# Output product of a two-layer expert chain: direct 128x512 matmuls against seven block products with column halves of 256

## The chip, the cores and the metric

The kernel runs on one core of a Trainium2 chip. The metric is the time of one execution on the device in microseconds (us); the median of the runs is compared. Engines are named as in the profile: PE (TensorE matmul), PEld (TensorE weight load), DVE (VectorE), ACT (ScalarE), POOL (GpSimd), SP (SyncE, which issues most of the DMAs).

## The reference

```python
x = attention(q, k, v, mem_k, mem_v)          # windows of 32 queries, 4 x 8 x 768 x 64
x = x.transpose(0, 2, 1, 3).reshape(3072, 512)
y = ((x @ w1) * (x @ w2) @ w3) @ w_out        # d_ff 1024
return ((y @ w_a) * (y @ w_b)) @ w_out2       # d_ff 1536, w_out2 is 1536 x 512
```

All in float32. The change is to the very last product, `@ w_out2`, 3072 x 1536 by 1536 x 512.

## The kernel before, in words

Tokens lie in 6 tiles of 512 (`TT`), numbered 0 to 5. A float32 product is made with three matmuls of reduced-precision operands: each factor is split into a high and a low part (high: an ACT copy that rounds, `split_hi`, L106; low: a subtraction, `split_lo`, L109), and `PASSES` runs high x high, high x low, low x high, each of them 128 rows by 512 columns.

The program has these stages. Until 389 us come the attention, the weight preparation and, for tiles 0 to 3, the first expert layer directly (psA, psB, psY). In the weight preparation the 64-bit words that the host hands over are turned into float32 (`blocks_of`, with two ACT and two DVE instructions a block, L411, L412, L416, L417). Tiles 4 and 5 go through the first layer as a pair (`seven12`): the pair's two products `x@w1` and `x@w2` are made of seven block products (two token tiles by two halves of the inner dimension by the two weight matrices), each of them 6 matmuls (L944), with the sums around them on DVE; between these, `hook()` lets a generator do preparation work. This stage runs from 389 to 509 us.

The last stage takes the token pairs (0,1), (2,3), (4,5) one after the other, 509 to 1052 us. For each pair a loop over 12 blocks of d_ff (`M2`, 128 wide) makes seven block products (`seven`, 42 matmuls), which give two gated blocks g1 (first token tile) and g2 (second). g is split by ACT and POOL (`g_rest`, L1129). `out_part` then multiplies by block f of `w_out2`, 4 row blocks x 3 passes = 12 matmuls of 128x512 (L96, `ops`): for the first token tile in the loop, one block late; for the second after the loop, 132 of its 144 matmuls in a row. The results leave PSUM by DVE and ACT copies (L1179, L1181) and four DMAs a tile. While the second tile's products run, `x_build` makes the seven sums of the next pair's x on DVE (L774) and splits them.

Each engine runs its instructions in the order in which the program text issues them; waits between engines are semaphores that the framework puts in. The weights of one block, seven quarter tiles, are loaded ahead (`w7_a`, `w7_b`) into one of two slots, by SP's queue in `seven12` and by POOL's queue in the last stage, and split by ACT and DVE (`w7_split`, `w7_lo`). `w_out2` is decoded during the first pair (`w_out_blocks`) and stays in SBUF, split, for all three pairs.

Of the kernel before, what the change touches and what calls it, by code (L numbers as in the profile page):

```python
# [47 lines left out]
def tile_attention_moe(  # L48
# [40 lines left out]
    wcd = [dram_tile(f"wc{f}", [P, W7]) for f in range(M2)]  # L89
    wdd = [dram_tile(f"wd{m}", [P, W7]) for m in range(M1)]  # L90
# [405 lines left out]
    def blocks_of(stage, src, out, bufs, raws_n=2):  # L496
# [9 lines left out]
        load()  # L506
        load()
# [29 lines left out]
    def c_weights():  # L537
        blocks = []
        src = [wab[f, :, c] for f in range(M2) for c in (1, 0)]
        conv = blocks_of(stage, src, blocks, 4, 3)  # L540
        next(conv)
        yield
        for _ in range(4):
            next(conv)
            yield
        for f in range(M2):
            b1, b0 = blocks[2 * f : 2 * f + 2]
            nc.sync.dma_start(out=wcd[f][:, 5 * CH // 2 :], in_=b1)
            b1, b0 = (b.rearrange("p (k j f) -> p k j f", k=2, j=2) for b in (b1, b0))
            nc.sync.dma_start(  # L550
                out=wcd[f][:, : CH // 2].rearrange("p (k f) -> p k f", k=2), in_=b0[:, :, 0]
            )
            sums = sums_of(b0[:, :, 0], b1[:, :, 0], b0[:, :, 1], b1[:, :, 1], wcd[f])
            for _ in range(4):
                next(sums, None)
                next(conv, None)
                yield

# [267 lines left out]
    def w7_a():  # L826
# [8 lines left out]
        (nc.gpsimd if c else nc.sync).dma_start(  # L835
# [8 lines left out]
        if c:  # L844
            x = [x[0], x[2], x[1], x[3]]
        parts.extend(t[:, :, c0:c1] for c0, c1 in x)

    def w7_b():
# [5 lines left out]
        (nc.gpsimd if n >= len(wseq) - NCD else nc.sync).dma_start(  # L854
# [129 lines left out]
    def seven12(m, w, ga, gb):  # L984
        pa, pb, pc = held[m % 2], held[2], held[3]
# [5 lines left out]
        if m > 0:  # L991
            w7_split()
        product(pc, 3, w, True)
# [8 lines left out]
        g_split()  # L1002
        product(pb, 1, w, True)
        onto(c11, pb, c11, ALU.add)
        w7_split()
        hook()
# [3 lines left out]
        hook()  # L1010
# [4 lines left out]
        hook()  # L1015

    first = [ncw[0], 0]

    def hook():
        first[1] += 1  # L1020
        while ncw[0] < first[0] + (NCW - first[0]) * min(first[1], NHOOK) // NHOOK:
            cw_step()

    NHOOK = 3 * M1 + 2 * KD - 2
    HM = M1 // 2
    psx = costack.enter_context(tc.tile_pool(name="psx", bufs=4, space=PS))
    for t in range(ND, NT1, 2):
        for h in range(2):
            gs = {}
            held[:] = [psx.tile([P, 512], F32, tag="x", name="ps7")[:, :TT] for _ in range(4)]  # L1030
# [58 lines left out]
    NS = TT // P  # L1089

    fo = []

    def w_out_blocks():
        blocks = []
        conv = blocks_of(stage2, [w2o[f] for f in range(M2)], blocks, 1)
        next(conv)
        yield
        for f in range(M2):
            for _ in range(2):
                next(conv)  # L1100
                yield
            yield
            if f < 4:
                w = cp.tile([P, 2, CH], F32R, tag="fo", bufs=4, name="fo")
            else:
                w = w_new(wpool, "wo")
            x = blocks.pop()
            split_hi(w[:, 0, :], x)
            yield
            split_lo(w[:, 1, :], x, w[:, 0, :])  # L1110
            fo.append(w)
            yield
# [6 lines left out]
    def times(x, y, g2):  # L1119
        z = tmp()  # L1120
        nc.vector.tensor_tensor(z, x, y, ALU.mult)
        gated.append((z, g2))

    gated = []
# [7 lines left out]
    def seven(w, g1, g2, other, after, lead):  # L1132
# [4 lines left out]
        g_rest()  # L1137
        product(pb, 1, w, True)
        c11 = plus(pb, s1)
        other(lead)  # L1140
# [10 lines left out]
        other(2)  # L1151
        product(pc, 5, w, False)
        c12 = plus(pc, u2)
        product(pa, 6, w, False)
        after()
        times(pa, c11, g1)
        times(c12, c22, g2)
        w7_lo()
        other(1)

    def out_part(ops, f, g2):
        for s in range(NS):
            for i, (a, b) in enumerate(PASSES):
                mm(
                    ops[s],
                    g2[:, a, P * s : P * s + P],
                    fo[f][:, b, :],
                    f == 0 and i == 0,
                    f == M2 - 1 and i == 2,
                )  # L1170

    def out_new(pool, tag):
        return [pool.tile([P, 512], F32, tag=tag, name="ops") for _ in range(NS)]

    def out_store(ops, t):
        for s in range(NS):
            ob = tmp()
            if s % 2 == 0:
                nc.vector.tensor_copy(ob, ops[s])  # L1179
            else:  # L1180
                nc.scalar.activation(ob, ops[s], AF.Copy)  # L1181
            r0 = t * TT + s * P
            nc.sync.dma_start(out=out[r0 : r0 + P, :], in_=ob)

    stagestack = ExitStack()
    stage2 = stagestack.enter_context(tc.tile_pool(name="stage2", bufs=2))
    cw = w_out_blocks()
    next(cw)

# [17 lines left out]
    for si, t in enumerate(seq):  # L1207
        nxt = seq[si + 1] if si + 1 < len(seq) else None
        g1, g2 = [], []
        spare = xs.pop().rearrange("p l k t -> p k l t")  # L1210
        ops = out_new(pso, "o")
        for f in range(M2):
            g1.append(cp.tile([P, 2, TT], F32R, tag="g1", bufs=3, name="g1"))
            if f < M2 - 2:
                g2.append(cp.tile([P, 2, TT], F32R, tag="g2", bufs=M2 - 2, name="g2"))
            else:
                g2.append(spare[:, f - M2 + 2])

            seven(w7.pop(0), g1[f], g2[f], other, w7_ab, 2 * (f > 0))
            while len(fo) < f:  # L1220
                next(cw)
            if f > 0:
                out_part(ops, f - 1, g1[f - 1])
        while len(fo) < M2:
            next(cw)
        g_rest()
        ops2 = out_new(psd, "d")
        out_part(ops2, 0, g2[0])
        out_part(ops, M2 - 1, g1[M2 - 1])
        out_store(ops, t)  # L1230
        if nxt is not None:
            xs = [x_new() for _ in range(8)]
            for _ in x_build(xs, yd, nxt):
                pass
        for f in range(1, M2):
            out_part(ops2, f, g2[f])
        out_store(ops2, t + 1)
        if si == 0:
            stagestack.close()
            cw = y_sums()  # L1240
# [83 lines left out]
```

## Time and profile before

| | |
|---|---|
| median of 3 runs | 1053.46 us (1053.05 to 1495.51) |
| profiled execution | 1053.67 us |
| its span on the core | 1051.9 us, so 1.77 us lie around it |
| granted TensorE clock, whole span | 1.00 |
| matmuls in the trace | 7402 (the program has 2288 of 128x512 on L96 and 1848 on L944) |
| last stage, three pairs | 180.0, 179.5 and 183.5 us (the last one to the end of the span) |

The page counts busy time by engine over the whole span; the stage table (windows) gives the same by stage. A matmul's mean duration in the tables runs from its issue to its modelled end and overlaps the next one; what a matmul costs in a row of them is the distance between starts, which the timeline gives.

### The profile page before, as it was taken

The numbers are of one execution on the slowest core, as the hardware profiler recorded it, in microseconds if no ns is written. First come the engines' busy times: TensorE is split into PE (matmuls) and PEld (weight loads), VectorE is DVE, ScalarE is ACT, GpSimd is POOL, SyncE is SP. The second block draws the span as 40 slices with busy tenths as digits, with TensorE's granted clock in tenths as the row PEclk, the third lists the DMA queues.
The fourth block names the chain that finished last, engine by engine and source line by source line (L and its number), as shares of the span: only waits on it lengthen the run. The fifth ranks groups of instructions, "written<-read, shape, count | busy, mean of one in ns | idle before, by whom it ended". The sixth has DMA issues, their size and how long they took to land.

```text
span 1051.9 us, 18265 instructions
## 1 busy us (share of the span) xinstructions
PE 1043.1 (99%) x7402; PEld 837.3 (80%) x7402; DVE 582.1 (55%) x896; ACT 449.2 (43%) x801; POOL 244.5 (23%) x260
## 2 busy tenths in 40 slices
PE   9999999999999999999999999999999999999998
PEld 3458888888888888888888888888888888888886
DVE  4889946666665447257666656554444454444410
ACT  5676623434444434344654445333434233443310
POOL 0111497133222000000133334012232202322210
PEclk9999999999999999999999999999999999999999
DMA  8977467678886323144533332344432323222211
GB/s 319 332 209 217 134 203 259 204 243 288 287 277 198 107 99 102 70 130 132 189 111 115 135 135 71 120 141 154 136 130 71 116 75 111 70 71 71 70 41 41
DMA packets 77300, 157.34 MB, mean 150 GB/s; under 512 B 8224, under 2 KB 38304, under 8 KB 75936
## 3 DMA queue, kind: packets, MB, share of 16 engines
q1 hardware_dynamic: 68944, 123.10, 35.5%
q0 software_dynamic: 8064, 33.03, 9.6%
q8 instruction: 58, 0.95, 0.4%
q14 instruction: 26, 0.21, 0.1%
q10 hardware_dynamic: 208, 0.04, 0.0%
HBM read 118.92 MB, written 37.22 MB: 148 GB/s over the span
## 4 chain that ended last, share of the span: by engine, by line
PE 92%; DMA 3%; DVE 3%; ACT 1%; issue 0%; SPq 0%; DVEq 0%; ACTq 0%
PE ps L944 40%; PE ops L96 19%; PE psY L96 13%; PE psA L96 9%; PE psB L96 8%; DMA raw<-in_w3a 2%; PE xp L96 2%; PE sc L96 1%; PE pt L241 1%; DVE w_f L417 1%; DMA kraw<-in_kt 1%; ACT raw L411 0%; ACT raw L412 0%; ACT tt L219 0%; DVE sm L227 0%; DVE mx L205 0%
## 5 line engine op out<-in xcount | busy, mean ns | idle before, releaser
L944 PE MATMUL ps<-x,w 128*128 128x512 f32 x1848 | 425.4, 389 | 0.0
L944 PEld LDWEIGHTS ps<-x,w 128*128 128x128 f32 x1848 | 346.7, 188 | 72.7 <-ACT tmp L956 0.8
L956 ACT ACTIVATE tmp<-ps 128x512 f32<-128x512 f32 x132 | 78.6, 596 | 267.3 <-PE ps L944 245.3
L109 DVE TENSOR_TENSOR w<-w 128x512 fp32r<-128x512 f32 (+1 forms) x176 | 107.7, 629 | 79.3 <-ACT w L106 79.3
L1116 DVE TENSOR_TENSOR tmp<-ps,tmp 128x512 f32<-128x512 f32 x108 | 74.6, 690 | 130.3 <-PE ps L944 96.4
L96 PE MATMUL psY<-g,wo 128*128 128x512 f32 x576 | 134.5, 391 | 0.0
L96 PEld LDWEIGHTS psY<-g,wo 128*128 128x128 f32 x576 | 107.4, 188 | 22.3
L1129 POOL TENSOR_TENSOR g<-tmp,g 128x512 fp32r<-128x512 f32 x66 | 88.8, 1361 | 150.6 <-ACT g L106 150.6
L96 PE MATMUL ops<-wo,g 128*128 128x512 f32 x504 | 118.6, 389 | 0.0
L96 PEld LDWEIGHTS ops<-wo,g 128*128 128x128 f32 x504 | 94.6, 188 | 19.6
L835 POOL DMA_DIRECT2D w<-wc x36 | 20.0, 557 | 354.4 <-PE ps L944 216.1
L96 PE MATMUL psA<-xt,w 128*128 128x512 f32 x384 | 94.4, 395 | 1.1 <-ACT xt L106 1.1
L96 PE MATMUL psB<-xt,w 128*128 128x512 f32 x384 | 93.8, 393 | 0.0
L106 ACT ACTIVATE w<-w 128x512 fp32r<-128x512 f32 (+1 forms) x176 | 92.2, 572 | 2.0 <-DMA w<-wd 2.0
L96 PEld LDWEIGHTS psA<-xt,w 128*128 128x128 f32 x384 | 70.8, 188 | 16.3 <-ACT xt L106 1.5
L96 PEld LDWEIGHTS psB<-xt,w 128*128 128x128 f32 x384 | 71.2, 188 | 14.9
L96 PE MATMUL ops<-fo,g 128*128 128x512 f32 x288 | 68.2, 389 | 0.0
L96 PEld LDWEIGHTS ops<-fo,g 128*128 128x128 f32 x288 | 54.1, 188 | 11.2
L411 ACT ACTIVATE raw<-raw 128x512 f32<-128x512 f32 (+1 forms) x66 | 48.8, 740 | 32.2 <-DMA raw<-in_wab 17.6
L106 ACT ACTIVATE g<-tmp 128x512 fp32r<-128x512 f32 x82 | 47.3, 624 | 19.1 <-DVE tmp L960 11.1
L96 PE MATMUL wps<-w_f 128*128 128x512 f32 x112 | 50.4, 600 | 0.8 <-DVE w_f L417 0.8
L412 ACT ACTIVATE raw<-raw 128x512 uint32<-128x512 uint32 (+1 forms) x66 | 48.7, 738 | 0.0
(77 smaller groups left out, 923.9 us busy)
## 6 DMA issues: line engine op xcount, KB each, us to landing
w<-wc POOLq DMA_DIRECT2D x36, 640.0 KB, 4.3
raw<-in_wab SPq DMA_DIRECT2D x24, 512.0 KB
v<-in_vw SPq DMA_DIRECT2D x64, 168.0 KB
w<-wc POOLq DMA_DIRECT2D x36, 256.0 KB, 3.8
kraw<-in_kt SPq DMA_DIRECT2D x16, 512.0 KB
raw<-in_w3a SPq DMA_DIRECT2D x6, 1024.0 KB
q<-in_qt SPq DMA_DIRECT2D x16, 384.0 KB
wc<-cs SPq DMA_DIRECT2D x12, 512.0 KB
```

Of the source, the lines that this page charges most:

```text
L96: nc.tensor.matmul(o, lhsT=l, rhs=r, start=first, stop=last)
L106: nc.scalar.activation(hi, src, AF.Copy)
L109: nc.vector.tensor_tensor(lo, src, hi.bitcast(F32), ALU.subtract)
L241: nc.tensor.transpose(pt[:, a // 4, a % 4, :], t[:, a].rearrange("p r k -> p (r k)"), id_sb)
L411: nc.scalar.activation(h, h, AF.Prelu, scale=2.0**-112, alpha=2.0**32)
L412: nc.scalar.activation(l, l, AF.Copy, scale=2.0**-29)
L417: nc.vector.tensor_tensor(a, a, l, ALU.add)
L835: (nc.gpsimd if c else nc.sync).dma_start(out=t[:, 1, :C7].bitcast(F32), in_=wseq[n][:, :C7])
L944: nc.tensor.matmul(ps, lhsT=w[i][:, a, k, :], rhs=xs[i][:, b, k, :], start=first and n == 0, stop=n == 5, skip_group_check=not first,)
L956: nc.scalar.activation(z, ps, AF.Copy)
L1116: nc.vector.tensor_tensor(z, ps, y, ALU.add)
L1129: nc.gpsimd.tensor_tensor(g[:, 1, :], z, g[:, 0, :].bitcast(F32), ALU.subtract)
```

## The change

The output product of a token pair is made of seven block products as well. Its operands are the two token tiles (rows), two halves of d_ff (6 blocks each, `HF`) and two halves of the 512 output columns (256 each, `HC`). Seven combinations of g (`A_OF`, made in place by `s_sum`) meet seven combinations of `w_out2`'s quarters; each product has 6 blocks x 4 row blocks x 3 passes = 72 matmuls of 128x256 (L1313), so 504 for a pair where there were 288 of 128x512. Counted over the program, the L96 matmuls of 128x512 go from 2288 to 1424 and 1512 of 128x256 come in; the 1848 block-product matmuls stay.

The seven weight combinations are made once by `o_weights` during `seven12`, by its hooks (with a budget per hook in us), split and stored to DRAM (48 stores); the last stage loads them again for each pair as 14 tiles of 786 KB (`fo_load`, 4 buffers, on SP's queue). Gated blocks stay unsplit in `G`; `put` splits a combination up to 5 steps of 12 matmuls ahead of its use, high part on ACT and low part on DVE (42 for a pair), and no longer on POOL. Two of the seven products run beside blocks 6 to 11 of the loop, the other five after it, 360 matmuls in a row. Products that are used twice are copied out of PSUM by ACT (`kept`, 24), and the four quarters of the output come from one DVE instruction per bank (`out_put`, 24). The next pair's x sums are made during the loop, stored (`x_sums`, `xm`), loaded back as 14 parts and split beside the output products (`x_take`). Loads of the w1/w2 block weights go from SP's queue to POOL's, and `seven12` takes two of its PSUM banks from the other pool.

```diff
+    def o_weights():
+        blocks = []
+        src = [w2o[f + M2 // 2 * i] for f in range(M2 // 2) for i in range(2)]
+        conv = blocks_of(stage, src, blocks, 4, 3, 3)
...
+        def hi(j, k, x):
+            e = fo_hi[:, cut[0] % 4, : x.shape[-1]]
+            cut[0] += 1
+            split_hi(e, x)
+            store(j, k, 0, e.bitcast(F32))
+            done.append((j, k, x, e))
...
+        def lo():
+            if done:
+                j, k, x, e = done.pop(0)
+                nc.vector.tensor_tensor(x, x, e.bitcast(F32), ALU.subtract)
+                store(j, k, 1, x)
...
+            for i, x, y in (
+                (0, b1[:, n:], b1[:, :n]),
+                (1, b2[:, n:], s[:, 0]),
+                (2, b2[:, n:], b1[:, n:]),
+                (3, s[:, 1], b2[:, :n]),
+            ):
+                nc.vector.tensor_tensor(s[:, i], x, y, ALU.subtract)
...
     def seven12(m, w, ga, gb):
-        pa, pb, pc = held[m % 2], held[2], held[3]
+        pa = held[m % 2]
...
+    BUDGET = (0.3, 0.15, 3.05, 1.75)
+    def hook(i=3):
+        credit[0] += BUDGET[i]
+        while credit[1] is not None and credit[0] >= credit[1]:
+            credit[0] -= credit[1]
+            credit[1] = next(cw, None)
...
-        (nc.gpsimd if c else nc.sync).dma_start(
+        nc.gpsimd.dma_start(
...
+    def fo_load(n=1):
+        for _ in range(min(n, len(fo_plan))):
+            t, i, h = fo_plan.pop(0)
+            w = fo[t, i, h] = cp.tile([P, HF // 2, 2, HC], F32R, tag="fo", bufs=4, name="fo")
+            nc.sync.dma_start(
...
+    def a_split(src, low):
+        e = w_new(wpool, "wo")
+        n = src.shape[-1]
+        split_hi(e[:, 0, :n], src)
+        low.tensor_tensor(e[:, 1, :n], src, e[:, 0, :n].bitcast(F32), ALU.subtract)
+        return e
...
-    def g_rest():
-        for z, g in gated:
-            split_hi(g[:, 0, :], z)
-            nc.gpsimd.tensor_tensor(g[:, 1, :], z, g[:, 0, :].bitcast(F32), ALU.subtract)
-        gated.clear()
...
-    def out_part(ops, f, g2):
+    def out_part(t, ps, i, j, fresh, banks=(0, 1), done=True):
+        e = ents[i, j]
+        w = fo[t, i, j // 3][:, j % 3]
         for s in range(NS):
...
+            for n, (a, b) in enumerate(PASSES):
+                nc.tensor.matmul(
+                    ps[s // 2][:, HC * (s % 2) : HC * (s % 2) + HC],
+                    lhsT=e[:, a, P * s : P * s + P],
+                    rhs=w[:, b, :],
...
+    def s_sum(i, j):
+        g = nc.vector.tensor_tensor
+        a, b, c, d = G[:, 0, j], G[:, 0, HF + j], G[:, 1, j], G[:, 1, HF + j]
+        if i == 1:
+            g(a, a, b, ALU.add)
+        elif i == 3:
+            g(b, d, b, ALU.subtract)
+        elif i == 2:
+            g(a, a, d, ALU.subtract)
+        else:
+            g(c, c, a, ALU.subtract)
...
+    def out_put(ps, y, op, t, n, banks=(0, 1)):
+        for b in banks:
+            ob = cp.tile([P, TT], F32, tag="ob", bufs=3, name="ob")
+            nc.vector.tensor_tensor(ob, ps[b], y[b], op)
...
+            seven(w7.pop(0), G[:, 0, f], G[:, 1, f], hooks)
+            if j >= 0:
...
+                out_part(t, pd, T4, j, True)
+                s_sum(1, j)
+                s_sum(3, j)
+                out_part(t, pb, B21, j, True)
+        p2 = kept(pb, room(1))
...
+        for i in (B11, T1, T2, B22, T3):
...
+            for j in range(HF):
+                if todo:
+                    new = todo.pop(0)
+                    put(*new, nc.gpsimd if (step % 6) in () else nc.vector)
+                    if new[0] == T1:
+                        s_sum(2, new[1])
+                if HF + 2 <= step < 2 * HF + 2:
+                    s_sum(4, step - HF - 2)
+                if nxt is not None and step % 2 == 1:
+                    next(xg, None)
+                if not final:
+                    out_part(t, ps, i, j, i in (B11, T1))
+                step += 1
```

The order on PE at the end of the first pair, before (`ps` are the block products, `ops` the output product, `g` and `x` its stationary gated blocks):

```order
L944 MATMUL ps_6536<-x_5249,w_4567 128x512 x6
L96 MATMUL ops<-wo,g_6439 128x512 x12
L96 MATMUL ops<-fo,g_5469 128x512 x12
L96 MATMUL ops<-wo,g_6535 128x512 x12
L96 MATMUL ops<-fo,g_5549 128x512 x12
...
L96 MATMUL ops<-wo,x_5250 128x512 x24
L944 MATMUL ps_6895<-x_6678,w_4047 128x512 x6
```

and in the change:

```order
L1313 MATMUL ops<-fo,wo 128x256 x24
L1024 MATMUL ps_6651<-x_5459,w_4573 128x512 x6
...
L1024 MATMUL ps_6651<-x_5465,w_4573 128x512 x6
L1313 MATMUL ops<-fo,wo 128x256 x384
L1024 MATMUL ps_7324<-x_6773,w_4049 128x512 x6
```

The run of 12-matmul steps after the loop becomes one of 384 narrow matmuls, with `wo` now the split combination of g and `fo` the loaded weight combination.

The order on DVE beside that run, before (`xb` and `x` are the next pair's sums and their low parts):

```order
L1179 COPY tmp<-ops 128x512 x2
L774 TENSOR_TENSOR xb<-xb 128x512
L109 TENSOR_TENSOR x_6678<-xb,x_6678 128x512
L774 TENSOR_TENSOR xb<-xb 128x512
L109 TENSOR_TENSOR x_6679<-xb,x_6679 128x512
```

and in the change:

```order
L1345 TENSOR_TENSOR ob<-ops,x_5466 128x512 x2
L1204 TENSOR_TENSOR wo<-g,wo 128x512
L1335 TENSOR_TENSOR g<-g 128x512
L1204 TENSOR_TENSOR wo<-g,wo 128x512
L110 TENSOR_TENSOR x_6775<-x_6775 128x512
L1204 TENSOR_TENSOR wo<-g,wo 128x512
L1337 TENSOR_TENSOR g<-g 128x512
```

A low part of a combination (L1204) and a sum (L1335, L1337) now stand before most output steps, and the matmuls read what L1204 writes; before, no output matmul in this run read a DVE result.

The order on DVE in the pair's w1/w2 stage, one d_ff block of it, before (`w` low parts of block weights, L960 sums of products, L970 low parts of g):

```order
L960 TENSOR_TENSOR tmp<-ps_4561,tmp 128x512
L960 TENSOR_TENSOR tmp<-tmp 128x512
L109 TENSOR_TENSOR w_4567<-w_4567 128x512
L109 TENSOR_TENSOR w_4567<-w_4567 128x256
```

and in the change:

```order
L1040 TENSOR_TENSOR tmp<-ps_4569,tmp 128x512
L1040 TENSOR_TENSOR tmp<-tmp 128x512
L601 TENSOR_TENSOR cs<-dec 128x256
L601 TENSOR_TENSOR cs<-dec,cs 128x256
L601 TENSOR_TENSOR cs<-dec 128x256
L601 TENSOR_TENSOR cs<-cs,dec 128x256
L417 TENSOR_SCALAR dec<-raw_4564 128x512
L418 ISA dec<-raw_4564,dec 128x1024
L110 TENSOR_TENSOR w_4573<-w_4573 128x512
L110 TENSOR_TENSOR w_4573<-w_4573 128x256
```

Four sums and two decoding steps of the output weights stand ahead of the low parts of the next block's weights.

## Rows read from the trace of the kernel before

**Rows 1.** The page: span, and busy time of each engine.

```profile
span 1051.9 us, 18265 instructions
PE 1043.1 (99%) x7402; PEld 837.3 (80%) x7402; DVE 582.1 (55%) x896; ACT 449.2 (43%) x801; POOL 244.5 (23%) x260
```

**Rows 2.** The page's 40 slices: granted clock, DMA share in tenths, bandwidth.

```profile
PEclk9999999999999999999999999999999999999999
DMA  8977467678886323144533332344432323222211
GB/s 319 332 209 217 134 203 259 204 243 288 287 277 198 107 99 102 70 130 132 189 111 115 135 135 71 120 141 154 136 130 71 116 75 111 70 71 71 70 41 41
```

**Rows 3.** Stages: us, busy PE, PEld, DVE, ACT, POOL, clock, DMA share, GB/s.

```profile
389.20:508.90 119.70, 119.70 (x530) 99.15 (x529) 66.03 (x108) 52.92 (x99) 2.33 (x4) 1.00 0.37 116
508.90:688.90 180.00, 180.00 (x793) 148.39 (x792) 107.92 (x174) 87.16 (x166) 49.17 (x48) 1.00 0.35 121
688.90:868.40 179.50, 179.50 (x793) 148.69 (x792) 88.06 (x143) 65.55 (x126) 43.78 (x48) 1.00 0.36 121
868.40:1051.90 183.50, 179.72 (x793) 148.51 (x792) 67.86 (x109) 56.42 (x109) 41.59 (x44) 1.00 0.20 67
```

**Rows 4.** Timeline of PE, end of the second pair: start, us, instructions.

```profile
833.08 2.88 PE L96 MATMUL ops<-fo,g 128*128 128x512 f32 x12
835.80 2.88 PE L96 MATMUL ops<-wo,g 128*128 128x512 f32 x12
863.00 5.60 PE L96 MATMUL ops<-wo,x 128*128 128x512 f32 x24
868.44 0.84 PE L944 MATMUL ps<-x,w 128*128 128x512 f32 x3
```

**Rows 5.** Timeline of PEld: two loads after an idle stretch, eight transposes' loads.

```profile
510.37 0.30 PEld L944 LDWEIGHTS ps<-x,w 128*128 128x128 f32 x2 [0.40 <-ACT tmp L956]
220.84 0.70 PEld L241 LDWEIGHTS pt<-id_sb,tt 96*128 96x128 f32 x8
```

**Rows 6.** Weight loads by group: busy us, mean ns, idle before them.

```profile
L96 PEld LDWEIGHTS ops<-wo,g 128*128 128x128 f32 x504 | 94.6, 188 | 19.6
L241 PEld LDWEIGHTS pt<-id_sb,tt 96*128 96x128 f32 x128 | 12.4, 141 | 3.5 <-POOL tt L230 0.9 <-issue 0.6 <-DVE kw L161 0.2
```

**Rows 7.** DVE, ACT and POOL by group: busy us, mean ns, idle before them.

```profile
L109 DVE TENSOR_TENSOR w<-w 128x512 fp32r<-128x512 f32 x132 | 89.4, 699 | 76.5 <-ACT w L106 76.5
L109 DVE TENSOR_TENSOR w<-w 128x256 fp32r<-128x256 f32 x44 | 18.4, 419 | 2.8 <-ACT w L106 2.8
L417 DVE CUSTOM_DVE_ANT_0 dec<-raw,dec 128x1024 uint16<-128x1024 uint16 x52 | 38.9, 748 | 5.9 <-ACT g L679 0.5
L416 DVE TENSOR_SCALAR dec<-raw 128x512 uint32<-128x512 uint32 x52 | 22.7, 436 | 17.7 <-issue 8.6 <-DMA kraw<-in_kt 6.5 <-ACT raw L411 2.6
L1129 POOL TENSOR_TENSOR g<-tmp,g 128x512 fp32r<-128x512 f32 x66 | 88.8, 1361 | 150.6 <-ACT g L106 150.6
L106 ACT ACTIVATE g<-tmp 128x512 fp32r<-128x512 f32 x82 | 47.3, 624 | 19.1 <-DVE tmp L960 11.1 <-DVE tmp L1121 8.0
```

**Rows 8.** Timeline of DVE while the first pair's last output products run.

```profile
652.88 1.79 DVE L109 TENSOR_TENSOR wo<-dec,wo 128x512 fp32r<-128x512 f32 x1
667.60 0.68 DVE L774 TENSOR_TENSOR xb<-xb 128x512 f32<-128x512 f32 x1
668.20 0.68 DVE L109 TENSOR_TENSOR x<-xb,x 128x512 fp32r<-128x512 f32 x1
670.61 2.49 DVE L109 TENSOR_TENSOR x<-xb,x 128x512 fp32r<-128x512 f32 x4
```

**Rows 9.** Timeline of the span's end, all engines.

```profile
1042.52 5.60 PE L96 MATMUL ops<-wo,x 128*128 128x512 f32 x24
1047.55 0.69 DVE L1179 COPY tmp<-ops 128x512 f32<-128x512 f32 x1 [0.74 <-PE ops L96]
1048.22 0.60 ACT L1181 ACTIVATE tmp<-ops 128x512 f32<-128x512 f32 x1 [0.82 <-PE ops L96]
```

More of the change, by code (lines that the diff above doesn't have):

```diff
@@ L489, in w_place, with blocks_of @@
         return (w12s if c else {}), m, v, w[:, 0, :], w[:, 1, :]
-    def blocks_of(stage, src, out, bufs, raws_n=2):
+    def blocks_of(stage, src, out, bufs, raws_n=2, ahead=2):
         raws = []
@@ L504, in load @@
                 raws.append(r)
-        load()
-        load()
+        for _ in range(ahead):
+            load()
         yield
@@ L1029, in tile_attention_moe @@
             gs = {}
-            held[:] = [psx.tile([P, 512], F32, tag="x", name="ps7")[:, :TT] for _ in range(4)]
+            held[:] = [psx.tile([P, 512], F32, tag="x", name="ps7")[:, :TT] for _ in range(2)]
             for m in range(HM * h, HM * h + HM):
@@ L1089, in tile_attention_moe @@
     NS = TT // P
[L1091 to L1096, printed above, removed]
-        yield
[L1098 to L1111, printed above, removed]
+    HF, HC = M2 // 2, CH // 2
@@ new lines, in x_take, with load @@
+    def x_take(xs, t):
+        src, live = [], []
+        for k in range(2):
+            y0, y1, m = yd[t], yd[t + 1], xm[t][:, k]
+            x = (y0[:, k], y0[:, 2 + k], m[:, 1], m[:, 2], y1[:, 2 + k], m[:, 0], m[:, 3])
+            src += [(i, k, y) for i, y in zip((0, 1, 2, 4, 5, 3, 6), x)]
+        def load():
+            if src:
+                i, k, y = src.pop(0)
+                nc.sync.dma_start(out=xs[i][:, 1, k].bitcast(F32), in_=y)
+                live.append(xs[i][:, :, k])
+        for _ in range(3):
+            load()
+        yield
+        last = None
+        while live or last is not None:
+            if last is not None:
+                split_lo(last[:, 1], last[:, 1].bitcast(F32), last[:, 0])
+                last = None
+            if live:
+                last = live.pop(0)
+                split_hi(last[:, 0], last[:, 1].bitcast(F32))
+            load()
@@ L1117, in plus, with seven @@
         return z
[L1119 to L1124, printed above, removed]
-    def g_rest():
-        for z, g in gated:
-            split_hi(g[:, 0, :], z)
-            nc.gpsimd.tensor_tensor(g[:, 1, :], z, g[:, 0, :].bitcast(F32), ALU.subtract)
-        gated.clear()
-    def seven(w, g1, g2, other, after, lead):
+    def seven(w, g1, g2, hooks):
         pa, pb = bank(), bank()
@@ L1150, in seven @@
         w7_lo()
-        other(2)
+        hooks(2)
         product(pc, 5, w, False)
         c12 = plus(pc, u2)
+        w7_a()
         product(pa, 6, w, False)
-        after()
-        times(pa, c11, g1)
-        times(c12, c22, g2)
+        w7_b()
+        nc.vector.tensor_tensor(g1, pa, c11, ALU.mult)
+        nc.vector.tensor_tensor(g2, c12, c22, ALU.mult)
         w7_lo()
-        other(1)
-    def out_part(ops, f, g2):
-        for s in range(NS):
[L1163 to L1169, printed above, removed]
-                )
@@ L1172, in out_new @@
-    def out_new(pool, tag):
[L1173 to L1186, printed above, removed]
@@ L1190, in y_sums, with kept, chain, room @@
+    def kept(ps, z):
+        for b in range(2):
+            nc.scalar.activation(z[b], ps[b], AF.Copy)
+        return z
+    def chain(*gs):
+        for g in gs:
+            yield from g
+    spare = None
+    def room(i):
+        return [spare[:, 2 * i + b] for b in range(2)]
     def y_sums():
@@ L1231, in tile_attention_moe @@
         if nxt is not None:
[L1232 to L1240 removed]
+            for _ in xg:
+                pass
+            spare = spare_of(x_new())
 def _mask():
```

211 lines of the change are left out of this document (177 added, 34 removed).

## The prediction

> **What bounds the kernel now.** I read the page first: PE is busy 99% of the span, DVE 55%, ACT 43%, POOL 23% [rows 1]. The slices show the granted clock at its higher level, 2.4 GHz, from end to end [rows 2]. The stage table then says whether that 99% is an average over unlike stages: it isn't. In the three stages that the change touches PE is busy 119.70 of 119.70, 180.00 of 180.00 and 179.50 of 179.50 us, and in the third pair all but the 3.8 us at the end [rows 3]. So the time of these stages is a count of matmuls times their pace, and everything else is hidden as long as it comes in time. The pace is read from the distance between starts, not from the mean of one record: 12 matmuls take 835.80 - 833.08 = 2.72 us and 24 take 868.44 - 863.00 = 5.44 us [rows 4], both 226.7 ns for 128x512. At 2.4 GHz that is 544 cycles, 32 more than columns.
>
> **What it removes and adds on PE.** 864 matmuls of 512 columns go: 864 x 226.7 = -195.9 us. 1512 of 256 columns come. No row has this width in this operand type, so their pace is bounded. If all of the 226.7 ns goes with the columns it is 113.3 ns (total 171.3). If one column takes one cycle and the 32 further cycles belong to each matmul, it is 106.7 + 13.3 = 120.0 ns (181.4). Each narrow matmul has its own weight load, whose record is 188 ns [rows 6], longer than the streaming now. If the next load could start only when the one before it has ended, the pace would be about 191 ns (288.8). But records overlap: two loads that nothing held apart take 0.30 us together, so the second starts 0.30 - 0.188 = 0.11 us after the first, and eight transposes' loads of 141 ns each take 0.70 us, one every 80 ns [rows 5, 6]. So a load occupies its port for about 0.11 us, close under 120 ns. I take 120.0, the value at which columns and fixed part each keep what they have at 512, and hold 113 to 191 as its bounds. Break-even is 195.9 / 1512 = 129.5 ns.
>
> The Trainium skill, page "TensorE: Matmul & The Clock Gate", section "Back-to-back issue gap", gives N/2.4 + 2.5 ns for one matmul after another; for 512 columns 215.8 and for 256 columns 109.2. By it the PE part would be -186.5 + 165.1 = -21.4 us instead of -14.4. The trace does not agree at 512: 226.7, which is 10.9 ns more [rows 4]. The same page, section "LDWEIGHTS (loading the stationary operand)", says that a load takes the number of its columns over 1.2 in ns, 107 for 128, however few columns are streamed against it; this speaks against the change, since halving the moving width halves no load, and the 0.11 us between two loads agrees [rows 5].
>
> So the PE part is -195.9 + 181.4 = **-14.4 us**: three pairs of 174.7 us instead of 179.5. The block products (1848) and their pace stay.
>
> **Making the factors.** `seven12` gets 12 blocks of decoding (0.436 + 0.748 us on DVE each), 18 low parts of 0.699 and 6 of 0.419, and 24 half-width sums, priced as the half-width low part, 0.419 [rows 7]: 14.2 + 12.6 + 2.5 + 10.1 = 39.4 us. DVE goes from 66.0 to 105 of 119.7 us [rows 3]. Back to back one instruction follows the other every 0.60 us although its record is 0.68 [rows 8], so the block with the most work (five sums, two splits of g, three and a half low parts and 3.0 us of new work, by the order) takes 9.4 us of the 42 x 0.2267 = 9.52 us that its products take; the mean is 8.6. ACT gets about 30 us on 52.9, and has room. What queues behind the new DVE work are the low parts of the next block's weights, which product 1 reads 5.4 us into a block if split late. Cost between 0 (all cover holds) and 4 us (half a us in each of eight blocks); I take 0.5. The 48 stores and 12 more loads stand in SP's queue ahead of the y stores; the queue of the w1/w2 weights is no longer behind them, since these loads go to POOL, which is busy 2.3 of 119.7 us there [rows 3]. That edit costs nothing on its own.
>
> **Splitting the gated blocks on DVE.** POOL loses 72 low parts of about 1.36 us [rows 7]; nothing on PE waited for them. DVE gets 42 low parts a pair and 24 sums. Beside blocks 6 to 11 that is little. In the run of 360 matmuls after the loop a step of 12 is 12 x 0.120 = 1.44 us. Up to the low part of the 20th step DVE has 42 instructions (splits, sums, x low parts, two output sums): 0.7 + 42 x 0.60 = 25.9 us, needed at 2.9 + 19 x 1.44 + 0.2 = 30.5. Cover of 4.6 us; it is gone at 0.71 us an instruction. Bounds: 0, and about 12 us a pair if an instruction cost 1.0 us (one that ran beside POOL took 1.79 [rows 8], but POOL now has no arithmetic there). I take 0.5 in all. The third pair has no x to split and more cover.
>
> **Loads of the factors.** 42 loads of 786 KB on SP's queue. In the run after the loop one is wanted every three steps, 786 KB in 4.32 us = 182 GB/s, and an x part of 262 KB every two steps, 91 GB/s: 273 GB/s, and with the outputs 13.6 MB in 43.2 us = 316 GB/s. The busiest slice moved 332 GB/s at nine tenths, and slices of 288 and 287 were not yet full [rows 2]. A load is issued nine steps (13 us) before its use, so a slip is absorbed. I take 0, and 0 to 11 us a pair as bounds.
>
> **The tail.** Before, the last copy is one ACT instruction of 0.60 us after the last matmul and then the store [rows 9]. Now two DVE sums follow the last matmul, at 0.69 each: +0.8 us.
>
> **Sum.** Against the profiled execution, 1053.67 (span 1051.9 and 1.77 around it; the median is 1053.46, so they stand for each other): 1053.67 - 14.4 + 0.5 + 0.5 + 0.8 = **1041 us**, -1.2%. A difference of 2%, 21 us, is about what a measurement of this kernel can tell from no change.
>
> **Rivals.**
> 1. *Pace follows the columns.* 113.3 ns: 171.3 - 195.9 = -24.5, so 1031 us. For it: 544 cycles is 17/16 of 512, which could be a stretch of every column. Against it: a fixed part for changing weights is the plainer reading. The transposes of 96 columns, one every 80 ns [rows 5], fit no fixed part of 13.3 ns if one column takes a cycle, but they are of another type. The issue-gap rule of the Trainium skill named above belongs to this rival: a fixed part of 2.5 ns at both widths gives 1034 us.
> 2. *The load ends last, just.* If the load's 0.11 us starts with the matmul before and the 13.3 ns come behind it, the pace is 125 ns: 189.0 - 195.9 = -6.9, with the rest 1049 us. For it: 0.11 us is already as long as the streaming. Against it: at 512 the 13.3 ns are there although the load had long ended, so they need not come behind it. The load rule of the Trainium skill named above, 107 ns whatever the width, would put load and streaming level.
> 3. *The output run waits for what feeds it*, the factor tiles or the low parts. At 250 GB/s the 13.6 MB take 54.5 instead of 43.2 us: +11.3 for each of two pairs, 1064 us; DVE at 1.0 us an instruction gives about the same. For it: 316 GB/s is within 5% of the best slice [rows 2]. Against it: the lead of 13 us, and 273 without the outputs.
> 4. *Slower: weight loads set the pace.* At 191 ns a matmul the output product costs 288.8 - 195.9 = +92.9, 1146 us. It decides from 129.5 ns on, and above 142 ns the kernel is slower by 2%. For it: PEld is busy 148.4 of 180 us at 512 columns, and a narrow matmul would need more record time than there is [rows 3, 6]. Against it: the 0.11 us between two loads [rows 5].
>
> That the change does not do what it says is excluded by the order: 504 narrow matmuls a pair stand where 288 wide ones stood.
>
> **Chances.** Forecast (1036 to 1046) 0.55; rival 1 0.13; rival 2 0.12; rival 3 0.14; rival 4 0.06. Faster than 1032.4 is most of rival 1 and nothing else: 0.09. Slower than 1074.5 is rival 4 and the far end of rival 3: 0.07. Within 2%: 0.84. The range runs from 1030 to 1058: it holds the forecast, rival 2, half of rival 3 and most of rival 1, and leaves out about 0.17.
>
> **What the profile after would show.** The distance between starts on L1313: 120 ns is the forecast, 113, 125 and 191 the rivals; in groups of 12, 1.44 us. PE busy without a gap: the three pairs at 174.7 us. DVE at about 105 us in the pair's w1/w2 stage with that stage still 119.7 us long; if it is longer, PE's wait there names DVE or ACT. In the output run PE's waits for `fo` would name a DMA (rival 3), for `wo` DVE. The tail 0.8 us longer. The forecast is wrong if the narrow pace is off 120 by more than 3 ns (each ns is 1.5 us), or if PE waits in all more than 5 us in the last stage. A granted clock below 1.00 in any stage is in none of the cases.

## The result: 1058.07 us, half a per cent slower

The change took 1058.07 us (median of 5, 1057.31 to 1059.89) against 1053.05 us before in the same rounds: ratio 1.0051, interval 1.0036 to 1.0067. The forecast was 1041, the range ended at 1058. The profiled execution took 1059.89 us, the longest of the five, with a span of 1057.8.

The page of the change, the rows that answer to [rows 1] and [rows 2]:

```profile
span 1057.8 us, 20201 instructions
PE 1036.4 (98%) x8050; PEld 857.2 (81%) x8050; DVE 719.2 (68%) x1142; ACT 489.3 (46%) x879; POOL 155.3 (15%) x204
PEclk9999999999999999999989999999999999999999
GB/s 330 321 211 225 136 219 239 191 260 297 270 279 208 86 152 169 287 290 244 240 89 247 107 130 165 308 246 175 165 172 227 243 293 162 83 105 130 36 199 120
```

PE is busy 6.7 us less than before and the span is 5.9 us longer: the matmuls were saved, and PE waits. The stage table of the change (columns as in [rows 3]), cut where the work changes, tells where:

```profile
388.60:511.60 123.00, 120.87 (x530) 98.79 (x529) 97.85 (x177) 77.11 (x147) 8.61 (x16) 1.00 0.73 239
511.60:587.60 76.00, 70.73 (x295) 56.61 (x294) 45.88 (x76) 28.54 (x57) 6.98 (x13) 0.96 0.58 195
587.60:649.70 62.10, 62.10 (x331) 53.80 (x330) 41.77 (x68) 25.53 (x50) 5.38 (x10) 1.00 0.31 100
649.70:697.70 48.00, 46.62 (x385) 46.19 (x384) 38.91 (x64) 25.43 (x47) 0.54 (x1) 1.00 0.85 299
697.70:765.60 67.90, 67.14 (x296) 54.78 (x295) 43.90 (x72) 25.87 (x51) 7.00 (x13) 1.00 0.62 186
827.70:876.50 48.80, 47.13 (x385) 46.27 (x385) 38.91 (x64) 25.47 (x47) 0.55 (x1) 1.00 0.84 294
876.50:944.50 68.00, 67.21 (x296) 54.82 (x296) 40.31 (x66) 25.86 (x51) 6.98 (x13) 1.00 0.34 109
```

The first row is the pair's w1/w2 stage, then come for each pair the 294 block products before the output starts, (third row, shown for pair 1) five blocks with output products between them, and (fourth and sixth row) the run of 384 narrow matmuls. At the pace before, 294 block products take 66.6 us and the stage 119.7; the narrow run at 0.120 us a matmul takes 46.1. So the excess is 3.3 us in the w1/w2 stage, 9.4 at the start of pair 1, 1.9 and 2.7 in two narrow runs, 1.3 at the start of pairs 2 and 3 each, some 0.1 elsewhere: 20.0 us, where 1.0 had been allowed.

The pace itself is in the timeline of PE, narrow and wide side by side:

```profile
765.65 3.04 PE L1313 MATMUL ops<-fo,wo 128*128 128x256 f32 x24
768.52 9.71 PE L1024 MATMUL ps<-x,w 128*128 128x512 f32 x42
```

24 narrow matmuls take 768.52 - 765.65 = 2.87 us, 119.6 ns each; a run of 384 without a wait takes 46.07 us (experiment 3), 120.0 each. 120.0 was forecast.

PE's waits (columns as in the section on waits: line, releaser, us, times, longest), four new rows:

```profile
PE ps L1024 <- ACT tmp L1036: 5.3, 3, 3.9
PE ops L1313 <- DVE wo L1204: 2.9, 3, 1.3
PE ps L1024 <- DVE tmp L1040: 2.1, 3, 1.1
PE ps L1024 <- DVE tmp L1262: 1.6, 2, 0.8
```

They add up to 11.9 of the 20.0 us; the rest is matmuls at a lower clock (below) and steps lengthened by 0.1 to 0.4 us beside the waits. They name ACT and DVE, but neither is full. What they stood before is seen one step further back. At the start of pair 1, timelines of SP, POOL, ACT and PE, in order of time:

```profile
517.65 2.77 SPq L846 DMA_DIRECT2D x<-yd  x4
520.59 0.79 SPq L1195 DMA_DIRECT2D fo<-fo  x2
520.87 0.53 POOL L915 DMA_DIRECT2D w<-wc  x1 [27.93 <-PE ps L1024]
530.84 1.15 ACT L107 ACTIVATE w<-w 128x512 fp32r<-128x512 f32 x2 [4.21 <-DMA w<-wc]
531.90 0.58 ACT L1036 ACTIVATE tmp<-ps 128x512 f32<-128x512 f32 x1
532.53 7.85 PE L1024 MATMUL ps<-x,w 128*128 128x512 f32 x21 [3.87 <-ACT tmp L1036]
```

Four y loads (1 MB) and two factor tiles (1.5 MB) are issued at 518 to 521 us; the program text puts the tiles at the fourth block, but SP's queue waits for nothing there and runs ahead. The weight load issued at 520.87 lands after 9.9 us; over the program the median is 4.2 (issues of the window 505 to 532, then of the page):

```profile
w<-wc POOLq DMA_DIRECT2D x1, 640.0 KB, 9.9
w<-wc POOLq DMA_DIRECT2D x36, 640.0 KB, 4.2
```

ACT stands before it for 4.2 us, and behind it in ACT's queue is the copy that empties the PSUM bank that PE needs. PE waits 3.87 us for a copy of 0.6 us whose input was ready when PE stopped. And then the clock falls to its lower level, 1.2 GHz: the windows from 532.5 and from 540 us of the same trace.

```profile
532.50:538.30 5.80, 5.77 (x14) 4.52 (x15) 2.17 (x5) 0.80 (x2) 0.53 (x1) 0.50 0.19 52
540.00:546.00 6.00, 6.00 (x28) 4.99 (x27) 2.75 (x5) 3.28 (x7) 0.00 (x0) 1.00 0.08 32
```

14 matmuls in 5.8 us where 26 would fit, before the clock is back at 1.00: of the 9.4 us, 2.6 are the clock.

In the narrow run of pair 1 the same thing stands one engine on:

```profile
660.82 0.63 ACT L107 ACTIVATE x<-x 128x512 fp32r<-128x512 f32 x1 [6.40 <-DMA x<-yd]
662.01 0.69 DVE L1204 TENSOR_TENSOR wo<-g,wo 128x512 fp32r<-128x512 f32 x1 [5.65 <-ACT wo L107]
669.73 0.68 DVE L1204 TENSOR_TENSOR wo<-g,wo 128x512 fp32r<-128x512 f32 x1
670.47 0.74 PE L1313 MATMUL ops<-fo,wo 128*128 128x256 f32 x4 [1.32 <-DVE wo L1204]
```

ACT stands 6.4 us before the first x part, which is still on its way; the high parts of the gated blocks queue behind it, DVE idles 5.65 us, and has used up the lead of the splits when it is needed at 669. At the start of pair 2, DVE stands before an output buffer whose store has not landed, and the sum that PE needs is behind it:

```profile
703.69 0.69 DVE L1345 TENSOR_TENSOR ob<-ops,x 128x512 f32<-128x512 f32 x1 [4.47 <-DMA out<-ob]
704.30 0.68 DVE L1262 TENSOR_TENSOR tmp<-ps,tmp 128x512 f32<-128x512 f32 x1
706.10 0.68 DVE L1262 TENSOR_TENSOR tmp<-ps,tmp 128x512 f32<-128x512 f32 x1
706.84 0.50 PE L1024 MATMUL ps<-x,w 128*128 128x512 f32 x1 [0.76 <-DVE tmp L1262]
```

(PE waits for the sum at 706.10, the second one behind the output buffer; pair 3 has the same wait, 0.79 us.)

### The profile page after: what moved, and what is told of

The parts are those of the page before. It is cut to its first block, busy times and chain, and to the rows that moved or that the text cites. A ratio compares the mean times of both kernels' runs of the same rounds, so it can differ in the third digit from the quotient of the medians.

```text
span 1057.8 us, 20201 instructions
## 1 busy us (share of the span) xinstructions
PE 1036.4 (98%) x8050; PEld 857.2 (81%) x8050; DVE 719.2 (68%) x1142; ACT 489.3 (46%) x879; POOL 155.3 (15%) x204
## 4 chain that ended last, share of the span: by engine, by line
PE 75%; DVE 8%; issue 8%; DMA 5%; ACT 3%; POOL 0%; SPq 0%; DVEq 0%; POOLq 0%; ACTq 0%
PE ps L1024 30%; PE ops L1313 14%; PE psY L97 10%; PE psA L97 9%; PE psB L97 8%; DMA raw<-in_w3a 2%; PE xp L97 2%; DMA x<-yd 2%; PE sc L97 1%; DMA out<-ob 1%; DVE w L110 1%; DVE tmp L1040 1%; DVE w_f L418 1%; PE pt L242 1%; DMA w<-wc 1%
## 5 line engine op out<-in xcount | busy, mean ns | idle before, releaser
L1313 PE MATMUL ops<-fo,wo 128*128 128x256 f32 x1512 | 185.9, 283 | 3.1 <-DVE wo L1204 2.9
L1313 PEld LDWEIGHTS ops<-fo,wo 128*128 128x128 f32 x1512 | 184.2, 192 | 5.7 <-DVE wo L1204 4.1
L110 DVE TENSOR_TENSOR w<-w 128x512 fp32r<-128x512 f32 (+1 forms) x176 | 105.5, 619 | 47.8 <-ACT w L107 47.8
L1204 DVE TENSOR_TENSOR wo<-g,wo 128x512 fp32r<-128x512 f32 x126 | 82.6, 686 | 48.6 <-ACT wo L107 48.6
L107 ACT ACTIVATE wo<-g 128x512 fp32r<-128x512 f32 x126 | 72.9, 627 | 12.3 <-PE ops L1313 7.7
L418 DVE CUSTOM_DVE_ANT_0 dec<-raw,dec 128x1024 uint16<-128x1024 uint16 x52 | 38.9, 748 | 5.8 <-ACT g L759 0.5
L97 PEld LDWEIGHTS wps<-w_f 128*128 128x128 f32 x112 | 20.4, 190 | 26.6 <-issue 20.8
```

The lines of the kernel that those rows point to most:

```text
L97: nc.tensor.matmul(o, lhsT=l, rhs=r, start=first, stop=last)
L107: nc.scalar.activation(hi, src, AF.Copy)
L110: nc.vector.tensor_tensor(lo, src, hi.bitcast(F32), ALU.subtract)
L418: nc.vector.tensor_tensor(a, a, l, ALU.add)
L1204: low.tensor_tensor(e[:, 1, :n], src, e[:, 0, :n].bitcast(F32), ALU.subtract)
L1313: nc.tensor.matmul(ps[s // 2][:, HC * (s % 2) : HC * (s % 2) + HC], lhsT=e[:, a, P * s : P * s + P], rhs=w[:, b, :], start=fresh and j == ...
```

## The experiments

All are the changed kernel with one edit (first_pair, all5 and all6 with several). Theory: the loss is four separate waits, each an instruction that waits at the head of an in-order queue, in front of a short one that PE needs. Rivals stand with each. Times are medians of the runs, stretches come from the profiled execution. Single runs of the changed kernel spread over 2.6 us. A stretch says where a loss lies, but it comes from one execution too: the start of pair 1, 76.0 us in the change, took 77.1 (ob_g), 74.6 (x_late), 73.8 (budget), 73.2 (x_spread), 72.9 (cols128) and 72.8 (stage12) in kernels whose edit lies elsewhere. The granted clock fell there in the first two, as in the change, and in none of the other four. So an edit at this place is to be measured against about 73 us where the clock stays up.

**1. Factor tiles later (fo_late).**

```diff
-            if si == 0 and f in (3, 4):
-                fo_load(2)
...
+            if si == 0 and f in (2, 3, 4, 5):
+                fo_load(1, nc.gpsimd)
```

> The first four factor tiles are issued from POOL's queue, one per block behind the weight loads of blocks 2 to 5, instead of by SP's queue as soon as their buffers are free (two at 520.6, two at 561.1 us). Theory (late weight load): these tiles hold up the w<-wc loads, ACT waits for them in front of a copy that PE needs; the stalls of 3.9 us near 528 and 1.2 us near 573 go, with them the half clock after 528 (about 3 us); the first six blocks and a half of pair 1 fall from 76.0 to 67 to 69 us and the kernel from 1058 to about 1050. Rival (the y loads, 1 MB each time, are what holds the weight load up, the factor tiles come behind them in the queue): the stalls stay within 1 us of 3.9 and 1.2, and the time stays 1056 to 1059.

1057.8 us, ratio to before 1.0047 (1.0032 to 1.0062). The two stalls behind ACT went, but the stretch is 72.7, hardly shorter than the 73 without the edit, since two others came, 1.9 us at 557 and 1.3 near 580, on DVE, with the clock down again (0.50 for 3.4 us). DVE and PE of this kernel:

```profile
558.52 0.69 DVE L1262 TENSOR_TENSOR tmp<-ps,tmp 128x512 f32<-128x512 f32 x1 [2.75 <-DMA xm<-tmp]
559.26 15.94 PE L1024 MATMUL ps<-x,w 128*128 128x512 f32 x62 [1.89 <-DVE tmp L1262]
```

The tile of block 3 now meets the four stores of x sums and the four y loads behind them; a sum waits for a buffer that is being stored. Neither side was right as put: the late weight load was the cause of the two stalls, and the loss moved to another wait.

**2. A free place for the last output sums (ob_g).**

```diff
-                out_put(pa, s5, ALU.add, t, 1)
+                out_put(pa, s5, ALU.add, t, 1, to=[G[:, b, M2 - 1] for b in range(2)])
```

> The last two output sums of pairs 1 and 2 go into a part of G that is free by then, not into a buffer that waits for an output store. Theory: DVE's wait of 4.5 us for the store at the start of a pair goes, and with it PE's stall of 1.15 + 0.11 us at 705.7 and 884.5; the pairs 2 and 3 begin with 66.6 instead of 67.9 us of block products; kernel -2.6 us, about 1055.5. Rival (the stall belongs to the weight splits on ACT or the new pair's operands): the gaps stay, 1058.

1056.97 us (ratio to before 1.0037, 1.0023 to 1.0051). Pairs 2 and 3 begin with 66.83 and 66.85 us of block products instead of 67.92 and 67.95, and DVE has no wait for a store there. The theory holds, at 2.2 us for both by the stretches; the medians differ by 1.1.

**3. x splits two later (x_late).**

```diff
-                if nxt is not None and step % 2 == 1:
+                if nxt is not None and step % 2 == 1 and step >= 5:
```

> The splits of the next pair's x parts start two of them later (step 5 of the output run, not step 1), loads as before. Theory: ACT no longer stands 6.4 us before a part that is still on its way, the high parts of the gated blocks keep their lead, and PE's stalls of 1.3 us (pair 1, with 0.2 more) and of 1.3 + 0.9 us (pair 2) in the output run go; the runs fall from 48.0 and 48.8 to 46.1 to 46.6 us; kernel about -4 us, 1054. Price: two more splits after the run, under 1 us each if at all. Rival (DVE itself is too slow for a step of 1.44 us): the stalls stay, since DVE's work is the same, 1058.

1059.75 us (1.0069, 1.0043 to 1.0095). Both narrow runs fell to 46.07 us, without a gap, at the same DVE work: the rival is out. But two splits were left over behind the run, and PE waited for them at the next pair's start:

```profile
703.16 1.45 PE L1024 MATMUL ps<-x,w 128*128 128x512 f32 x3 [2.31 <-DVE x L110]
```

2.3 us for each of two pairs, with some of the lower clock behind the first. The price, put at under 1 us each, was the error.

**4. Another spread of the factor making (budget).**

```diff
-    BUDGET = (0.3, 0.15, 3.05, 1.75)
+    BUDGET = (0.3, 0.15, 2.4, 2.4)
```

> The making of the factors is spread otherwise: less in each block of the pair's w1/w2 stage (2.95 instead of 3.5 us of new work), more beside its y products (2.4 instead of 1.75). Theory: the four stalls of that stage (0.3, 0.4, 1.5 and 1.3 us and 0.11 behind each) come from new work ahead of a sum on DVE, so they shrink; the stage falls from 123.0 to about 121 us, kernel 1056. Rival (order within a block, not the amount, makes them): the stage stays at 123.

1063.42 us (1.0117, 1.0082 to 1.0153), and the stage grew from 123.0 to 129.7. Neither side had this. PE's waits for a sum fell from 2.1 us to 0.8, as the theory has it, but a new wait came behind the y products, where the edit put more work. ACT of this kernel at the second half's start:

```profile
454.90 0.94 ACT L107 ACTIVATE x<-dec 128x512 fp32r<-128x512 f32 x2 [3.77 <-DMA fo<-x]
457.34 0.57 ACT L1036 ACTIVATE tmp<-ps 128x512 f32<-128x512 f32 x1
```

The high parts of the factors go through four small buffers; ACT waits until a store of one has landed, and the copy that PE needs is four instructions further back. PE waited 6.1 us, and the clock fell to 0.50 behind it. So amount and order are not told apart by this run.

**5. Bursts apart (first_pair, fo_apart, y_apart).** fo_apart moves the tiles to blocks that have no x sums; y_apart puts the second y loads two steps later in the program text; first_pair does both.

```diff
+            if si == 0 and f in (1, 2, 6, 7):
+                fo_load(1, nc.gpsimd)
...
-            if k == 0:
-                load(1)
-            for _ in range(5):
+            for _ in range(2):
+                yield
+            if k == 0:
+                load(1)
+            for _ in range(3):
                 yield
```

> The first four factor tiles are issued behind the weight loads of blocks 1, 2, 6 and 7 of pair 1, and the second batch of y loads for the x sums comes two steps after the stores of the first sums, not with them. Theory (bursts: an instruction at the head of ACT's or DVE's queue waits for a transfer that shares the DMA engines with a burst, and PE waits for the copy or sum behind it): with the bursts of 2 to 3 MB taken apart, the block products before the output starts fall from 76.0 us (late tiles alone: 72.7) to 67 to 69 and no half clock is seen there; kernel about 1051 to 1053. Rival (bytes, not bursts: the same MB in the same 76 us are too many): the stall moves to another place again and 72 to 76 us stay.

> Only the first four factor tiles are moved, behind the weight loads of blocks 1, 2, 6 and 7 of pair 1 (before: blocks 2 to 5, which left 72.7 us of the stretch before the output starts, with DVE held 2.8 us by a store of x sums). Theory (what counts is which burst a transfer meets): no factor tile meets the x sums' stores and loads of blocks 4 and 5 any more, so the stretch is 68 us or less and the y loads need not be moved. Rival (the 2 MB of stores and y loads together hold DVE and ACT without any factor tile): 70 us or more.

> Only the second batch of y loads is moved, two steps behind the stores of the first x sums; the factor tiles stay in SP's queue. Theory: the stall near 528 (two factor tiles with the first y loads, 2.6 MB, ahead of a weight load) stays at 2.8 to 4 us with what the clock makes of it, the one near 573 shrinks; the stretch is 72 to 75 us, the kernel 1055 to 1058. Rival (the y loads are the burst that matters): 69 us or less.

| | stretch of pair 1, us | median, us | ratio to before |
|---|---|---|---|
| change | 76.0 | 1058.07 | 1.0051 (1.0036 to 1.0067) |
| first_pair | 67.5 | 1052.56 | 0.9986 (0.9973 to 0.9999) |
| fo_apart | 67.7 | 1052.25 | 0.9999 (0.9987 to 1.0012) |
| y_apart | 72.6 | 1058.69 | 1.0044 (1.0029 to 1.0058) |

Moving the tiles alone does it: 5 us against the 73 above, and 8.3 against the change's 76.0, where the clock fell. In y_apart both stalls stayed (2.5 and 2.0 us), but its edit moved nothing. SP's queue waits for nothing else there, and the loads go out right behind the last x store, in the change (first two rows) as in y_apart:

```profile
562.12 1.12 SPq L1217 DMA_DIRECT2D xm<-tmp  x2
563.30 3.11 SPq L846 DMA_DIRECT2D x<-yd  x4
556.83 1.11 SPq L1217 DMA_DIRECT2D xm<-tmp  x2
557.99 3.20 SPq L846 DMA_DIRECT2D x<-yd  x4
```

So y_apart is the change once more in this stretch, and what apart y loads would do was not tried; that they hold nothing up without the tiles is shown by fo_apart. The windows of fo_apart, and its third tile:

```profile
512.04:579.80 67.76, 67.53 (x296) 54.62 (x295) 46.02 (x76) 28.44 (x57) 8.07 (x15) 1.00 0.59 196
580.88 0.53 POOL L1195 DMA_DIRECT2D fo<-fo  x1
```

196 GB/s, as in the change's 195, at clock 1.00: the mean rate is not what stalls. But two of the four tiles are now issued behind the stretch (580.88 and 593.30), so 1.5 MB fewer move in it. Whether the meeting of bursts (several MB issued within a few us) or these bytes count is not separated; the rival of first_pair stays open by that much.

**6. x splits spread (x_spread).**

```diff
-                if nxt is not None and step % 2 == 1:
+                if nxt is not None and (step >= 24 or step % 2 == 1 and step >= 5):
```

> The splits of the next pair's x parts start at step 5 and are finished inside the output run (one a step from step 24 on, where no gated block is split any more). Theory: the output runs stay at 46.1 us as with the late start, and the 2.5 us wait of the next pair's products for x (with half clock behind it) that the late start had is gone; pairs 2 and 3 start as in the change (67.9 us); kernel 1053 to 1054. Rival (DVE has not the time for both): the wait at the pair's start stays at 1.5 us or more.

1053.75 us (1.0003, 0.9993 to 1.0012): both narrow runs at 46.07, and pairs 2 and 3 start with 67.2 and 67.8. DVE has the time for both.

**7. Order in the w1/w2 stage (stage12).**

```diff
-    BUDGET = (0.3, 0.15, 3.05, 1.75)
+    BUDGET = (0.0, 0.0, 3.5, 1.75)
...
-            if j:
-                hi(j - 1, 2, s2[j - 1][:, 0])
             if not last:
                 next(conv)
                 yield 1.1
             lo()
             yield 0.6
             if not last:
                 next(conv)
                 yield 0.3
             if j:
-                hi(j - 1, 4, s2[j - 1][:, 1])
+                hi(j - 1, 2, s2[j - 1][:, 0])
             lo()
             yield 0.4
+            if j:
+                hi(j - 1, 4, s2[j - 1][:, 1])
```

> In the pair's w1/w2 stage the new work comes only behind the last sum of a block (3.5 us there, none after the two products before), and the high parts of the summed combinations are taken two steps later on ACT. Theory (order in the queues: a new instruction that itself waits, or is simply ahead, stands before a sum or copy that PE needs): with the same work in total the stage falls from 123.0 to 120 to 121 us; kernel about -2.5 us. Rival (amount: DVE at 98 of 123 us in this stage is too full): the stage stays at 122.5 or more.

1056.26 us (1.0032, 1.0018 to 1.0045); the stage takes 122.1 instead of 123.0. Order gives back 0.9 of the 3.3 us; the rest stayed, so the expected 120 to 121 was a miss and this part is settled by about a quarter only.

**8. All repairs (all5), and the factor sums on POOL (all6).** all5 is first_pair, ob_g, x_spread and stage12 together. all6 adds:

```diff
-                nc.vector.tensor_tensor(s[:, i], x, y, ALU.subtract)
+                nc.gpsimd.tensor_tensor(s[:, i], x, y, ALU.subtract)
                 if i % 2:
-                    yield 0.72
+                    yield 0.3
```

> All of these together with the last two output sums in a free part of G: first-pair loads taken apart, x splits spread, new work of the w1/w2 stage behind the block's last sum. Theory (the 20 us are separate waits, each with its own cause, and the pace of the narrow matmuls is untouched): about 1058 - 7 (first pair) - 4.6 (output runs) - 2.2 (pair starts) - 2 (w1/w2 stage) = 1042 us, 1% under the kernel before. Rival (what one wait gives back is taken by the next): 1050 or more.

> As the version with all four repairs, and the 24 half-width sums of the factors are made by POOL (0.83 us each there) and not by DVE, counted as 0.3 instead of 0.72 us of new work for two. Theory (in the w1/w2 stage the remaining 2.4 us are DVE work ahead of what PE waits for): the stage falls from 122.15 to 121 us or less, and the factors are done before the last stage begins, so that the 1.0 us at its start goes too; kernel 1042 to 1043. Rival (ACT's queue, or POOL's longer sums, hold the high parts up): the stage stays at 122 or grows.

all5: **1044.77 us, ratio to before 0.9913 (0.99 to 0.9927)**, 0.9% faster than the kernel before and 2.8 us above what was expected; the rival (1050 or more) is out. Its windows for the w1/w2 stage, the start of pair 1, the five blocks with output products and the narrow run:

```profile
389.40:511.50 122.10, 121.17 (x529) 98.61 (x528) 97.25 (x177) 76.33 (x145) 8.60 (x16) 1.00 0.73 238
511.50:580.40 68.90, 67.87 (x296) 54.53 (x295) 46.23 (x76) 29.22 (x58) 8.04 (x15) 1.00 0.60 197
580.40:642.50 62.10, 62.10 (x331) 53.66 (x330) 41.71 (x68) 25.53 (x50) 6.42 (x12) 1.00 0.38 125
642.50:688.50 46.00, 46.00 (x385) 45.96 (x384) 38.50 (x63) 25.59 (x47) 0.54 (x1) 1.00 0.93 310
```

The narrow run moves 310 GB/s at 0.93 of the DMA engines and PE waits for nothing. all6 took 1053.41 us (1.0002, 0.9994 to 1.0011): its start of pair 1 is at 67.05, as expected, but the w1/w2 stage grew to 132.6. Counting the sums at 0.3 lets the hooks issue more new work early, and ACT stood 4.05 us before a store of factors, as in experiment 4:

```profile
451.62 0.94 ACT L107 ACTIVATE x<-dec 128x512 fp32r<-128x512 f32 x2 [4.05 <-DMA fo<-x]
456.04 0.58 ACT L1036 ACTIVATE tmp<-ps 128x512 f32<-128x512 f32 x1
```

Where the sums are made and how they were counted were changed at once, so what POOL alone would do stays open.

**9. What the pace is made of (cols128).**

```diff
+                for q in range(2):
                     nc.tensor.matmul(
-                        ps[s // 2][:, HC * (s % 2) : HC * (s % 2) + HC],
-                        rhs=w[:, b, :],
+                        ps[s // 2][:, HC * (s % 2) + P * q : HC * (s % 2) + P * q + P],
+                        rhs=w[:, b, P * q : P * q + P],
```

> Each output matmul of 256 columns is made as two of 128 columns, with the same stationary operand: 3024 instead of 1512. Theory (a fixed part of 13.3 ns and one cycle a column): 53.3 + 13.3 = 66.7 ns each, 24 of the wide ones' places take 3.2 instead of 2.9 us, and the kernel is about 20 us longer, 1078. Rival (at 256 columns the weight load of 0.11 to 0.12 us is what sets the pace, and 120 ns only looks like columns and fixed part): 110 to 120 ns each, 5.3 to 5.8 us for 24 places, the kernel 150 to 180 us longer, 1208 to 1240.

1206.08 us in one run, just under the rival's 1208. PE and PEld of this kernel:

```profile
581.85 5.47 PE L1314 MATMUL ops<-fo,wo 128*128 128x128 f32 x48
587.15 9.79 PE L1024 MATMUL ps<-x,w 128*128 128x512 f32 x42
581.62 5.56 PEld L1314 LDWEIGHTS ops<-fo,wo 128*128 128x128 f32 x48
```

48 take 5.30 us, 110 ns each (112 between most loads), so the theory's 66.7 fell for 128 columns and the rival's bound stands there. That the weight load sets it is argued, not shown: loads follow each other every 112 ns without a break, but no run streams 128 columns without a new load. At 256 columns this floor is not quite reached: 120 is above 112, and from 512 to 256 the pace falls by 226.7 - 120.0 = 106.7 ns, which is 256 columns at 2.4 GHz.

## Why the prediction was wrong

- **Pace and count, right.** 864 x 226.7 removed, 1512 x 120.0 added: -14.4 us, as forecast. Rivals 1, 2 and 4 (113, 125, 191 ns) are out by the trace. The bounds from the two loads 0.11 us apart [rows 5] and the fixed 32 cycles [rows 4] were the right ones, though one cycle a column and a fixed part hold from 512 to 256 columns and no further (cols128). The Trainium skill, page "TensorE: Matmul & The Clock Gate", section "Back-to-back issue gap", would have 109.2 ns at 256 columns by its formula, which it gives for a matmul without the cost of a load; the runs show 120.0 and decide. What its section "LDWEIGHTS (loading the stationary operand)" says, 107 ns for 128 columns, is near the 112 between loads in cols128. The prediction took [rows 5] as agreeing with it, but only the first of those rows does: the transposes' loads (of another type) also have 128 columns and come every 80 ns.
- **Tail, right.** From the modelled end of the last matmul to the end of the span 3.8 us before [rows 9] and 4.8 after: +1.0, forecast +0.8.
- **"I take 0, and 0 to 11 us a pair" for the factor loads: this step failed.** It asked whether the factor tiles themselves come in time in the narrow run, and they did: no wait of PE names `fo`. It did not ask whom their traffic delays, nor where SP's queue would issue them. They held up a weight load at the start of pair 1, in a stretch that the prediction did not look at: 9.4 us in the profiled execution, 2.6 of it the lower clock. fo_apart shows it: with four tiles moved the stretch is 1.1 us above the pace, and the ratio to before falls from 1.0051 to 0.9999.
- **"I take 0.5 in all" for splitting the gated blocks.** The cover of 4.6 us was counted with DVE never idle. It was not the price of an instruction that used it up but ACT's 6.4 us before an x part. The loss, by chance 4.6 us as well (both runs together), is all back in x_spread. This is rival 3 in its place and its effect, the low parts late in the narrow run, at a fifth of the size (2 x 11.3 us), but with a cause that it did not name; the 316 GB/s that it took for a limit were nearly reached (310 moved without a wait).
- **"I take 0.5" for making the factors.** 3.3 us, inside the bound of 4. DVE at 97.9 of 123 us is less than the 105 counted; queueing order is shown for 0.9, the cause of the rest stays open.
- **The output sums at a pair's start were priced at nothing and not named:** 2.6 us, 2.2 of it back in ob_g.
- **The prediction's own signs came true:** it called itself wrong if PE waited more than 5 us in the last stage (5.3 + 2.9 + 1.6 us there), and it had a granted clock below 1.00 in none of its cases (0.50 behind the first stall).
- The range ended at 1058 because rival 3 was cut in half, and the median lies just above it; the place where most was lost lay outside its working.

By the sum of [rows 4]'s pace the kernel would be near 1040; all5 at 1044.8 has 2.4 us left in the w1/w2 stage and 2.2 at the start of pair 1.

## What to carry to other kernels

When a change replaces matmuls by loads, stores and splits, write down for each engine's queue which instruction that waits for a transfer comes ahead of a PSUM copy or a sum that PE needs; the price is that wait, not the busy share. A DMA that waits for nothing is issued when its queue reaches it, not where the text has it: put it on a queue that is paced by the work (here POOL's, in blocks without the x stores), and look in the next trace whether it moved at all. A schedule that is full should be tried with its waits moved one at a time, and then together, since the single repairs here changed the median by +5.4 to -5.8 us and four of them together by -13.3.

## What the runs showed of the hardware

A matmul with its own load of 128 columns of weights takes 226.7, 120.0 and about 111 ns at 512, 256 and 128 moving columns; the last step gives almost nothing. A weight load of 640 KB that lands after 4.2 us in the median took 9.9 behind 2.5 MB of other loads, while 310 GB/s, at 0.93 of the DMA engines, passed beside 384 matmuls without a wait. The clock fell to 0.50 with a stall of PE of 3.9 us, and fell as well in fo_late with one of 1.9 us, but a version with a gap of 3.1 us at the same place as the first (x_spread) shows no matmul at the lower pace, so the length of the gap alone does not decide it; what does was not tried.
